# Two small layer-norm operations made on GpSimd instead of VectorE, with a new backlog guard and new order rules in the kernel's own scheduler

## The chip, the cores and the metric

The kernel runs on one core of one Trainium2 chip. The metric is the device time of one launch in microseconds (us), as the median of repeated runs.

The engines are TensorE (PE, with weight loads as PEld), ScalarE (ACT), VectorE (DVE), GpSimd (POOL) and SyncE (SP, which issues transfers).

## The reference, cut to what matters

```python
x = A_x                                          # 1 x 2048 x 640, bf16
xn = _layernorm(x, axis=-1)                      # (x - mean) / sqrt(var + eps)
q = (xn @ wq).reshape(1, 2048, 32, 20)           # 32 heads of 20
k = xn @ wk                                      # one K and one V for all heads
v = xn @ wv
scores = einsum("bhqd,bkd->bhqk", q, k) * 20 ** -0.5
o = einsum("bhqk,bkd->bhqd", softmax(scores), v)
h = relu(xn @ w1 + b1) ** 2
out = x + o_heads_joined @ wo + h @ w2 + b2
```

Nearly all the work is the softmax: 32 heads x 2048 x 2048 scores, which are 2048 tiles of 128 x 512, each of which needs an exponential.

## The kernel before: the parts that the change and the argument touch

The kernel file holds a list scheduler. Every piece of work is an `op` with an engine, an assumed duration, its dependencies and a priority. While the program is built, the scheduler decides in which order each engine gets its operations. The engines then work through fixed queues in that order (a wait of 0.98 us at the head of one is followed up below).

The layer norm of one row tile `st` (128 of the 2048 sequence rows; there are 16 of them, called rows below):

```python
def rows(st):
    p = ROWP[st // 4]
    if st in ACTST:
        ...                                # both statistics passes on ScalarE, small operation on VectorE
    else:
        s1 = op(f"S{st}a", "DVE", 0.40, lambda e: e.bn_stats(...), [x_op[st]], prio=p)
        s2 = op(f"S{st}b", "DVE", 0.40, lambda e: e.bn_stats(...), [x_op[st]], prio=p)
        ag = op(f"AG{st}", "DVE", 0.19, lambda e: e.bn_aggr(...), [s1, s2], prio=p - 0.1)
        ve = op(f"VE{st}", "DVE", 0.08, lambda e: e.tensor_scalar(... scalar1=EPS ... op0=ALU.add), [ag], prio=p - 0.1)
        if st in POOLXN:
            s1 = op(f"NM{st}", "DVE", 0.08, lambda e: e.tensor_scalar(... scalar1=-1.0 ... op0=ALU.mult), [ag], prio=p - 0.1)
    pw = op(f"PW{st}", "POOL", 0.52, lambda e: e.tensor_tensor(... op=ALU.pow), [ve, c_half], lock=True, prio=st // 4)
    eng, dur = ("POOL", 0.87) if st in POOLXN else ("DVE", 0.36)
    xn_op[st] = op(f"XN{st}", eng, dur, lambda e: e.tensor_scalar(...), [pw, s1, x_op[st]], lock=True, prio=p - 0.2)
```

So `VE` adds the epsilon, `NM` negates the mean, `PW` takes the power -1/2 and `XN` normalises. Each normalised row is transposed on TensorE (`T`), copied to SBUF (`TE`), and feeds the products for K, Q and V. Score products (`QK`) need K and Q.

The scores go to one of two consumers. ScalarE takes two or three tiles at a time:

```python
return Op(f"ACT{st_['j']}", "ACT", 0.05 + 0.4267 * n, [lambda e: e.activation(out=PT[...], in_=ps[...], func=AF.Exp, ...)], deps)
```

VectorE and GpSimd take sets of four tiles: one VectorE operation `D1` a tile evicts the score from PSUM as an integer approximation of the exponential, and three more passes a set run on either engine. How many sets there are is not fixed; the scheduler opens a new one (`make_dqk`, `new_set`) when it finds room for it:

```python
def make_dqk(heads):
    opn = [s for s in sets[-NL:] if s["left"]]
    fb = pool_banks()
    if not fb or (len(fb) == 1 and behind()):
        return None
    s = next((s for s in opn if [h for h in s["left"] if h not in heads]), None)
    if s is None:
        if len(opn) >= par("NOPEN"):
            return None
        s = new_set()
```

`par(...)` looks a value up in `RULES`, a table with an entry for stages of 10 us of the schedule. Where TensorE would be idle, the scheduler puts in filler products that compute nothing that is used.

The softmax here doesn't subtract the row's maximum and nothing guards it: scores larger than these inputs give would overflow.

## Time and profile before

| | before |
|---|---|
| time, median of 3 | 705.39 us (705.05 to 706.08) |
| span of the profile | 703.6 us |
| score tiles on ScalarE, on VectorE and GpSimd | 1480, 568 (142 sets) |
| exponentials of 1024, of 1536 columns | 665, 50 |
| first exponential starts | 15.30 us |
| last exponential ends | 695.14 us |
| from there to the end (the tail) | 8.5 us |

The rows of the table come from the timeline and the groups of the trace; the prediction shows the lines. The way to read it: ScalarE's queue of exponentials is one long row without holes. The time is the start of that row, plus its length, plus the tail. A row has a length by count (0.904 us for each 1024-wide exponential, 1.330 us for each 1536-wide one, from start to start) and an excess over it, which I sum from the starts of all exponentials: 3.20 us before 40 us, 8.64 us after it.

### The profile page before, as it was taken

The page shows a single profiled execution, that of the slowest core. Times are in us where ns is not written, and L with a number is a line of the kernel's source. Part 1 is how long each engine was busy: PE and PEld are TensorE (multiplying, and loading weights), DVE is VectorE, ACT ScalarE, POOL GpSimd, SP SyncE. Part 2 cuts the span into 40 slices and gives each one's busy share as a digit, 9 for nine tenths or more (in the row PEclk, how much of TensorE's full clock was granted, in tenths as well). Part 3 has the DMA queues.
Part 4 walks back from the last instruction along what each step waited for, and adds up shares of the span by engine and source line. Part 5 has one row for each costly group of instructions (what it writes and reads, how often), then busy time and mean ns, then how long its engine had stood idle before and what let it go on. Part 6 is the DMA issues. An engine that isn't in the chain of part 4 may idle for free.

```text
span 703.6 us, 22608 instructions
## 1 busy us (share of the span) xinstructions
PE 695.0 (99%) x9780; PEld 216.0 (31%) x9781; DVE 645.9 (92%) x1125; ACT 687.5 (98%) x739; POOL 427.3 (61%) x268
## 2 busy tenths in 40 slices
PE   8999999999999999999999999999999999999997
PEld 4422223233322223332322222323333222233333
DVE  7789999999999998989998998899899999999894
ACT  6899999999999999999999999999999999999995
POOL 4767556567566764666568765766665675644253
PEclk9999999999999999999999999999999999999999
DMA  6325422233337701211101001111112100031201
GB/s 201 98 70 153 115 78 58 81 97 80 84 85 160 162 20 25 55 40 37 52 18 40 23 22 28 29 47 26 46 42 51 36 22 23 20 106 51 55 26 39
DMA packets 42016, 44.00 MB, mean 63 GB/s; under 512 B 15540, under 2 KB 32772, under 8 KB 41788
## 3 DMA queue, kind: packets, MB, share of 16 engines
q1 hardware_dynamic: 39132, 36.93, 19.2%
q0 software_dynamic: 2208, 5.25, 3.9%
q8 instruction: 76, 1.25, 0.7%
q10 hardware_dynamic: 576, 0.38, 0.2%
q14 instruction: 24, 0.20, 0.1%
HBM read 28.03 MB, written 14.91 MB: 61 GB/s over the span
## 4 chain that ended last, share of the span: by engine, by line
ACT 95%; PE 4%; DMA 1%; DVE 0%; SPq 0%; issue 0%; DVEq 0%
ACT PT L910 94%; PE ps L367 3%; DMA x_sb<-in_A_x_dram 1%; PE ps L540 1%; ACT xnT L477 0%; ACT OC L421 0%; DVE out_sb L1164 0%; PE ps L568 0%; SPq L384 0%; ACT OC L422 0%; SPq L391 0%; PE ps L510 0%; PE ps L496 0%; DVEq L227 0%; DVE PT L1164 0%
## 5 line engine op out<-in xcount | busy, mean ns | idle before, releaser
L910 ACT ACTIVATE PT<-ps 128x1024 bf16<-128x1024 f32 (+1 forms) x715 | 677.1, 1219 | 3.8 <-PE ps L367 3.8
L1083 DVE TENSOR_SCALAR tmore<-ps 128x512 uint16<-128x512 f32 x568 | 367.4, 683 | 31.7 <-PE ps L367 28.2
L1101 POOL TENSOR_SCALAR tmore<-tmore 128x2048 uint16<-128x2048 uint16 x109 | 206.4, 1900 | 171.1 <-PE ps L367 62.3
L367 PE MATMUL ps<-qT,kT 20*128 20x512 bf16 x2048 | 281.7, 384 | 1.9 <-ACT PT L910 0.8
L1101 POOL TENSOR_SCALAR x_sb<-tmore 128x2048 uint16<-128x2048 uint16 x100 | 189.3, 1902 | 79.4 <-DVE x_sb L1101 24.2
L367 PEld LDWEIGHTS ps<-qT,kT 20*128 20x128 bf16 x2048 | 71.6, 91 | 280.4 <-ACT PT L910 233.1
L367 PE MATMUL ps<-PT,vx 128*32 128x512 bf16 x1480 | 136.9, 386 | 0.2 <-ACT PT L910 0.2
L1101 DVE TENSOR_SCALAR x_sb<-tmore 128x2048 uint16<-128x2048 uint16 x135 | 96.1, 745 | 0.1
L367 PE MATMUL ps<-x_sb,vxs 128*32 128x512 bf16 x940 | 83.2, 382 | 0.0
L367 PE MATMUL ps<-xnT,w_sb 128*32 128x512 bf16 x960 | 77.2, 384 | 0.1
L367 PE MATMUL ps<-w_sb,big 128*32 128x320 bf16 x1536 | 74.5, 302 | 0.0
L367 PE MATMUL ps<-tmore,vxs 128*32 128x512 bf16 x764 | 69.6, 382 | 0.0
L1101 DVE TENSOR_SCALAR tmore<-tmore 128x2048 uint16<-128x2048 uint16 x82 | 61.5, 770 | 0.1
L367 PE MATMUL ps<-tmore,vx 128*32 128x512 bf16 x568 | 55.7, 382 | 0.0
L367 PEld LDWEIGHTS ps<-PT,vx 128*32 128x32 bf16 x1480 | 34.9, 94 | 62.1 <-issue 53.6
L367 PEld LDWEIGHTS ps<-w_sb,big 128*32 128x32 bf16 x1536 | 32.1, 95 | 29.3 <-issue 22.2
L648 DVE TENSOR_SCALAR hT_tmp<-ps,b1col 128x512 bf16<-128x512 f32 x48 | 35.8, 746 | 3.4 <-PE ps L367 2.7
L367 PE MATMUL ps<-xnT,wq_sb 128*32 128x512 bf16 (+1 forms) x480 | 33.7, 356 | 0.2 <-DVE tmore L1083 0.2
L367 PE MATMUL ps<-wo_c,OC 128*32 128x320 bf16 x608 | 30.9, 301 | 0.0
L367 PEld LDWEIGHTS ps<-x_sb,vxs 128*32 128x32 bf16 x940 | 21.3, 95 | 19.9 <-issue 13.4
L367 PEld LDWEIGHTS ps<-xnT,w_sb 128*32 128x32 bf16 x960 | 17.6, 94 | 26.7 <-issue 22.4
L367 PEld LDWEIGHTS ps<-tmore,vxs 128*32 128x32 bf16 x764 | 18.1, 95 | 16.4 <-issue 11.5
(81 smaller groups left out, 259.4 us busy)
## 6 DMA issues: line engine op xcount, KB each, us to landing
xbd<-b2d SPq DMA_DIRECT2D x16, 320.0 KB, 4.4
xbd<-in_A_x_dram POOLq DMA_DIRECT2D x8, 640.0 KB, 5.8
xr<-xbd SPq DMA_DIRECT2D x32, 160.0 KB, 2.4
w_sb<-in_B_w_dram SPq DMA_DIRECT2D x8, 480.0 KB, 4.4
big<-OR SPq DMA_DIRECT2D x71, 40.0 KB
big<-drs SPq DMA_DIRECT2D x71, 40.0 KB
out_dram<-out_sb SPq DMA_DIRECT2D x15, 160.0 KB, 1.8
qT<-QCr SPq DMA_DIRECT2D x108, 20.0 KB
```

What stands on the lines that cost most here:

```text
L367: return lambda e: e.matmul(out_, l, r, start=start, stop=stop, tile_position=tp)
L540: return [(lambda e, dt=dt: e.transpose(out=psbf(bk)[:, dt * 128:(dt + 1) * 128], in_=xn_sb[:, st, dt:D:DT], identity=ident[:])) for dt in ...
L648: o = Op(f"RL{qc}_{f}", "DVE", 0.66, [lambda e: e.tensor_scalar(out=hT_tmp[:, k % 2, :], in0=ps[:, bk, :], scalar1=b1col[:, f:f + 1], scal ...
L910: return Op(f"ACT{st_['j']}", "ACT", 0.05 + 0.4267 * n, [lambda e: e.activation(out=PT[:, s0:s0 + n, :], in_=ps[:, b0:b0 + (n - 1) * db + ...
L1083: d1 = op(f"D1_{n}_{i}", "DVE", 0.60, lambda e: e.tensor_scalar(out=L[:, cs].bitcast(U16), in0=ps[:, bank, :], scalar1=XA, scalar2=XB, op0 ...
L1101: p = op(f"P{j}_{n}", eng, 0.60 if eng == "DVE" else 1.86, lambda e, T=T, j=j, two=two: e.tensor_scalar(out=T.bitcast(U16), in0=L.bitcast( ...
```

## The change

The intent: VectorE, over 90% busy, is relieved of 18 small operations, GpSimd gets them, the scheduler sees VectorE's backlog before it hands out more tiles (the guard), and the table of order rules is chosen anew for that.

```diff
+DJIT = 9.0
-RULES = {3: {'PVA': 2.1, ...                      # 51 stages, cut
+RULES = {1: {'PVA': 0.95, ...                     # 60 stages, other values, cut
-PRIO = {'NM15': 2.12, 'NM10': 2.88, 'PW2': 0.96}
-NBEF = {'AG4': 10.21, 'NM7': 11.5, 'Qe0_1': 10.11, 'PW12': 25.33}
+PRIO = {'XN1': 0.13}
+NBEF = {'S4a': 6.0, 'AG5': 10.23, 'PW1': 4.94}
-QEACT = (0, 1, 2, 3)
+QEACT = (0, 1)
-FFN0 = 0.3
+FFN0 = 0.6
-ACTST = (2, 5, 6)
-POOLXN = (2, 7, 9, 10, 11, 13, 14, 15)
+ACTST = (0, 2, 4)
+POOLXN = (7, 9, 10, 11, 13, 14, 15)
@@ rows
+            small, pp = (("DVE", 0.08), p - 0.1) if st < 4 else (("POOL", 0.13), st // 4 - 0.5)
-                ve = op(f"VE{st}", "DVE", 0.08, ... prio=p - 0.1)
+                ve = op(f"VE{st}", *small, ... prio=pp)
-                    s1 = op(f"NM{st}", "DVE", 0.08, ... prio=p - 0.1)
+                    s1 = op(f"NM{st}", *small, ... prio=pp)
@@ make_dqk
             if not fb or (len(fb) == 1 and behind()):
                 return None
+            if max(free["DVE"], free["PE"]) + sum(o.dur for o in dve_q if o.frees is not None) > free["PE"] + 0.43 + par("DJIT"):
+                return None
```

The line of `DEFAULTS` that makes `DJIT` known to `par` is left out. `DJIT` is the backlog that the guard allows, `PRIO` and `NBEF` set the priority and the earliest time of single operations, `FFN0` the earliest place of the feed-forward part. `ACTST` are the rows whose statistics ScalarE takes, `POOLXN` those that GpSimd normalises, `QEACT` those whose first Q copy ScalarE makes.

More of the change, by code (lines that the diff above doesn't have):

```diff
@@ L80 @@
 KEEP = 1
-RULES = {3: {'PVA': 2.1, 'PVD': 2.1, 'R3': 1, 'PP': 0.9},
-         4: {'PVA': 2.1, 'PVD': 2.1, 'R3': 1, 'PP': 0.9, 'WARM': 0.78},
-         5: {'D1P': 1, 'MPRIO': 0.5, 'PBIAS': 2.5},
-         6: {'D1P': 1, 'MPRIO': 0.5, 'PBIAS': 2.5, 'ND': 1, 'QKP': 0},
-         7: {'DQP': 2.05, 'URG': 2, 'PVD': 2.1, 'BEHIND': -0.3},
-         8: {'WARM': 0.85, 'DQP': 0.95},
-         10: {'ND': 1, 'NOPEN': 3},
-         11: {'ND': 1, 'NOPEN': 3},
-         12: {'EPS': 0.12},
-         13: {'EPS': 0.06, 'EVP': 0.3},
-         15: {'PBIAS': 0},
-         17: {'EPS': 0.06},
-         18: {'EPS': 0.12},
-         19: {'WARM': 0.78, 'PBIAS': 2.5, 'IDLE': 0.3},
-         21: {'PBIAS': 0, 'KEEP': 0},
-         23: {'EPS': 0.12},
-         25: {'R3': 1, 'EVP': 0.3},
-         26: {'R3': 1, 'EVP': 0.3, 'IDLE': 0.3, 'PVD': 2.1},
-         28: {'EPS': 0.12, 'URG': 3},
-         29: {'EPS': 0.12, 'URG': 3, 'KEEP': 3, 'EVP': 1.1, 'ND': 3},
-         31: {'PBIAS': 1, 'D1P': 1, 'PVD': 1.05},
-         32: {'PBIAS': 1, 'D1P': 1, 'PVD': 1.05, 'DGAP': 0.8, 'DQP': 0.95, 'SQP': 2, 'R3': 1},
-         36: {'PP': 0.9, 'BEHIND': -0.1, 'EVP': 0.3, 'PBIAS': 1.5},
-         37: {'URG': 3, 'JIT': 1.0, 'PVD': 1},
-         38: {'SQP': 0.7, 'URG': 3},
-         39: {'PP': 2.5},
-         40: {'PBIAS': 1},
-         41: {'PBIAS': 1, 'DGAP': 1.5, 'SQP': 0.7},
-         42: {'PBIAS': 1, 'DGAP': 1.5, 'SQP': 2, 'NOPEN': 3, 'ND': 2, 'PVD': 1},
-         43: {'PBIAS': 1, 'DGAP': 1.5, 'SQP': 2, 'NOPEN': 3, 'ND': 2, 'PVD': 1, 'R3': 9},
-         44: {'WARM': 0.78, 'KEEP': 3, 'DLAST': 7.5},
-         45: {'DGAP': 0.8, 'KEEP': 1, 'D1P': 3},
-         48: {'PBIAS': 1},
-         49: {'PBIAS': 1, 'R3': 1},
-         50: {'PBIAS': 1, 'R3': 1},
-         53: {'DLAST': 3.5},
-         54: {'DLAST': 3.5, 'EPS': 0, 'EVP': 0.3},
-         55: {'DLAST': 3.5, 'EPS': 0, 'EVP': 0.3, 'ND': 1},
-         56: {'EVP': 2, 'MPRIO': 1.0},
-         57: {'R3': 1, 'ND': 1},
-         58: {'BEHIND': -0.1, 'EPS': 0, 'PP': 4, 'R3': 1},
-         59: {'BEHIND': -0.1, 'EPS': 0, 'PP': 4, 'R3': 1, 'DRATE': 0.95, 'DLAST': 10, 'PVA': 2.1},
-         60: {'EVP': 1.1},
-         61: {'EVP': 1.1, 'SQP': 0.7},
-         62: {'EVP': 1.1, 'SQP': 0.7, 'KEEP': 3, 'R3': 1, 'NOPEN': 2, 'D1P': 3},
-         64: {'PP': 0.9, 'DRATE': 0.8},
-         65: {'R3': 1},
-         66: {'R3': 1},
-         67: {'EPS': 0.12, 'PVA': 1.05},
-         68: {'R3': 0},
-         69: {'R3': 0, 'JIT': 1.1}}
@@ new lines @@
+DJIT = 9.0
+RULES = {1: {'PVA': 0.95, 'EPS': 0.2, 'DGAP': 0.8},
+         2: {'JIT': 0.9},
+         3: {'JIT': 0.9, 'R3': 0},
+         5: {'EPS': 0.2, 'DJIT': 0.6},
+         6: {'SQP': 2, 'EPS': 0.06},
+         7: {'SQP': 2, 'EPS': 0.06},
+         8: {'DQP': 0.95, 'D1P': 1},
+         9: {'MPRIO': 1.0},
+         10: {'DRATE': 1.1, 'D1P': 1},
+         12: {'R3': 2, 'ND': 1, 'JIT': 1.0, 'MPRIO': 1.1},
+         13: {'NOPEN': 1, 'DRATE': 1.1},
+         14: {'NOPEN': 1, 'DRATE': 1.1, 'KEEP': 2, 'DLAST': 3.5},
+         15: {'R3': 1},
+         16: {'R3': 1, 'DJIT': 1.0, 'ND': 3, 'DRATE': 0.8, 'DGAP': 0.25},
+         17: {'R3': 1, 'DJIT': 1.0, 'ND': 3, 'DRATE': 0.8, 'DGAP': 0.25},
+         18: {'PP': 0.9, 'NOPEN': 1},
+         19: {'PP': 0.9, 'NOPEN': 1, 'EVP': 2, 'SQP': 1.5, 'DJIT': 9},
+         20: {'PP': 4, 'NOPEN': 1, 'EVP': 2, 'SQP': 1.5, 'DJIT': 9},
+         21: {'EVP': 2, 'URG': 2},
+         22: {'JIT': 0.82},
+         23: {'IDLE': 0.2, 'D1P': 3},
+         24: {'IDLE': 0.2, 'D1P': 3, 'PBIAS': 1.5, 'DRATE': 0.95},
+         25: {'DJIT': 0.6, 'DRATE': 0.95, 'URG': 4},
+         26: {'D1P': 1, 'PVA': 2.1, 'DGAP': 0, 'DRATE': 0.95},
+         27: {'JIT': 1.0, 'SQP': 0.7},
+         28: {'EPS': 0.06, 'IDLE': 0.5},
+         29: {'PP': 0.9, 'DRATE': 0.95, 'DLAST': 4.5},
+         30: {'NOPEN': 3, 'DQP': 2.05, 'EPS': 0.12},
+         38: {'DQP': 2.05, 'PBIAS': 2.5},
+         39: {'DQP': 2.05, 'PBIAS': 2.5, 'PP': 2.5, 'IDLE': 0.1, 'ND': 1, 'DRATE': 1.1},
+         40: {'DLAST': 2.5, 'R3': 1, 'EPS': 0.06, 'EVP': 0.3},
+         41: {'DLAST': 2.5, 'R3': 1, 'EPS': 0.03, 'EVP': 0.3, 'DJIT': 0.3},
+         42: {'DLAST': 2.5, 'R3': 1, 'EPS': 0.03, 'EVP': 0.3, 'DJIT': 0.3, 'PBIAS': 0.3},
+         43: {'IDLE': 2, 'DJIT': 9, 'DLAST': 2.5, 'DRATE': 0.95},
+         44: {'IDLE': 2, 'DJIT': 9, 'DLAST': 2.5, 'DRATE': 0.95, 'EPS': 0.12},
+         45: {'IDLE': 2, 'DJIT': 9, 'DLAST': 2.5, 'DRATE': 0.95, 'EPS': 0.12, 'SQP': 0.7, 'BEHIND': -0.3, 'KEEP': 1},
+         46: {'DGAP': 1.5, 'MPRIO': 1.1, 'BEHIND': 0.5},
+         47: {'DGAP': 1.5, 'MPRIO': 0.5, 'BEHIND': 0.5, 'PBIAS': 0.3, 'R3': 1, 'NOPEN': 2},
+         48: {'DGAP': 1.5, 'MPRIO': 0.5, 'BEHIND': 0.5, 'PBIAS': 0.3, 'R3': 1, 'NOPEN': 2, 'D1P': 0.5, 'DRATE': 1.1},
+         49: {'DGAP': 1.5, 'MPRIO': 0.9, 'BEHIND': 0.5, 'PBIAS': 0.3, 'R3': 1, 'NOPEN': 2, 'D1P': 3, 'DRATE': 1.1, 'DLAST': 3.5, 'EVP': 2},
+         50: {'DGAP': 1.5, 'MPRIO': 0.9, 'BEHIND': 0.5, 'PBIAS': 0.3, 'R3': 1, 'NOPEN': 2, 'D1P': 3, 'DRATE': 1.1, 'DLAST': 3.5, 'EVP': 2},
+         51: {'DGAP': 1.5, 'MPRIO': 0.9, 'BEHIND': 0.5, 'PBIAS': 0.3, 'R3': 1, 'NOPEN': 2, 'D1P': 3, 'DRATE': 1.1, 'DLAST': 3.5, 'EVP': 2, 'EPS': 0.06, 'PP': 4},
+         52: {'DGAP': 1.5, 'MPRIO': 0.9, 'BEHIND': 0.5, 'PBIAS': 2.5, 'R3': 1, 'NOPEN': 2, 'D1P': 1, 'DRATE': 1.1, 'DLAST': 3.5, 'EVP': 2, 'EPS': 0.06, 'PP': 4, 'SQP': 0.7, 'URG': 4},
+         53: {'DGAP': 1.5, 'MPRIO': 0.9, 'BEHIND': 0.5, 'PBIAS': 2.5, 'R3': 1, 'NOPEN': 2, 'D1P': 1, 'DRATE': 1.1, 'DLAST': 3.5, 'EVP': 1.1, 'EPS': 0.06, 'PP': 2.5, 'SQP': 0.7, 'URG': 4},
+         54: {'DGAP': 1.5, 'MPRIO': 0.9, 'BEHIND': 0.5, 'PBIAS': 2.5, 'R3': 1, 'NOPEN': 2, 'D1P': 1, 'DRATE': 1.1, 'DLAST': 3.5, 'EVP': 1.1, 'EPS': 0.06, 'PP': 2.5, 'SQP': 0.7, 'URG': 6, 'KEEP': 3},
+         55: {'DGAP': 1.5, 'MPRIO': 0.9, 'BEHIND': 0.5, 'PBIAS': 2.5, 'R3': 1, 'NOPEN': 2, 'D1P': 1, 'DRATE': 1.1, 'DLAST': 3.5, 'EVP': 1.1, 'EPS': 0.06, 'PP': 2.5, 'SQP': 0.7, 'URG': 6, 'KEEP': 3},
+         56: {'JIT': 0.82, 'MPRIO': 0.9, 'PP': 2.5},
+         57: {'JIT': 0.82, 'MPRIO': 0.9, 'PP': 2.5, 'WARM': 0.85, 'R3': 1, 'SQP': 0.7},
+         58: {'JIT': 0.82, 'MPRIO': 0.9, 'PP': 2.5, 'WARM': 0.85, 'R3': 1, 'SQP': 0.7},
+         59: {'DLAST': 4.5},
+         60: {'DLAST': 4.5, 'NOPEN': 2, 'MPRIO': 1.0},
+         61: {'DLAST': 4.5, 'NOPEN': 2, 'MPRIO': 1.0},
+         62: {'R3': 0, 'WARM': 0.78},
+         63: {'R3': 0, 'WARM': 0.78, 'NOPEN': 1, 'URG': 2},
+         64: {'R3': 0, 'WARM': 0.78, 'NOPEN': 1, 'URG': 2},
+         65: {'R3': 0, 'WARM': 0.78, 'NOPEN': 1, 'URG': 2},
+         66: {'R3': 0, 'WARM': 0.78, 'NOPEN': 1, 'URG': 2, 'D1P': 1, 'ND': 2, 'MPRIO': 0.9, 'DQP': 0.95},
+         67: {'R3': 9, 'WARM': 0.78, 'NOPEN': 1, 'URG': 2, 'D1P': 1, 'ND': 2, 'MPRIO': 0.9, 'DQP': 0.95},
+         68: {'R3': 9, 'WARM': 0.78, 'NOPEN': 1, 'URG': 2, 'D1P': 0.5, 'ND': 2, 'MPRIO': 0.9, 'DQP': 0.95, 'PBIAS': 1},
+         69: {'R3': 0, 'WARM': 0.78, 'NOPEN': 1, 'URG': 2, 'D1P': 0.5, 'ND': 2, 'MPRIO': 0.9, 'DQP': 0.95, 'PBIAS': 1}}
@@ L159 @@
 DEFAULTS = dict(EVP=EVP, PBIAS=PBIAS, MPRIO=MPRIO, DGAP=DGAP, DLAST=DLAST, DRATE=DRATE, BEHIND=BEHIND, IDLE=IDLE, URG=URG, NOPEN=NOPEN,
-                EPS=0.03, JIT=JIT, R3=R3, STATIC=STATIC, PVA=1, PVD=1, D1P=1, PP=4, SQP=2, DQP=3, QKP=0, ND=2, WARM=WARM, KEEP=KEEP)
+                EPS=0.03, JIT=JIT, R3=R3, STATIC=STATIC, PVA=1, PVD=1, D1P=1, PP=4, SQP=2, DQP=3, QKP=0, ND=2, WARM=WARM, KEEP=KEEP, DJIT=DJIT)
 class Ctr:
@@ L428, in rows @@
                 ag = op(f"AG{st}", "DVE", 0.19, lambda e: e.bn_aggr(out=mv[:, st, :], in_=stats6[:, st, :, :].rearrange("p a b -> p (a b)")), [s1, s2], prio=p - 0.1)
-                ve = op(f"VE{st}", "DVE", 0.08, lambda e: e.tensor_scalar(out=mv[:, st, 1:2], in0=mv[:, st, 1:2], scalar1=EPS, scalar2=None, op0=ALU.add), [ag], prio=p - 0.1)
+                ve = op(f"VE{st}", *small, lambda e: e.tensor_scalar(out=mv[:, st, 1:2], in0=mv[:, st, 1:2], scalar1=EPS, scalar2=None, op0=ALU.add), [ag], prio=pp)
                 opm = ALU.subtract
                 if st in POOLXN:
-                    s1 = op(f"NM{st}", "DVE", 0.08, lambda e: e.tensor_scalar(out=mv[:, st, 0:1], in0=mv[:, st, 0:1], scalar1=-1.0, scalar2=None, op0=ALU.mult), [ag], prio=p - 0.1)
+                    s1 = op(f"NM{st}", *small, lambda e: e.tensor_scalar(out=mv[:, st, 0:1], in0=mv[:, st, 0:1], scalar1=-1.0, scalar2=None, op0=ALU.mult), [ag], prio=pp)
                     opm = ALU.add
```

## The prediction

> **What bounds the kernel now.** I read four views in this order: the page's busy table, its chain of waits, the groups by shape, and the timeline of ScalarE over the first 40 us.
>
> ```profile
> span 703.6 us, 22608 instructions
> PE 695.0 (99%) x9780; PEld 216.0 (31%) x9781; DVE 645.9 (92%) x1125; ACT 687.5 (98%) x739; POOL 427.3 (61%) x268
> ...
> ACT 95%; PE 4%; DMA 1%; DVE 0%; SPq 0%; issue 0%; DVEq 0%
> ```
>
> Three engines are over 90% busy, so the busy table doesn't decide. The chain does: 95% of the span is ScalarE, nearly all of it on one line, the softmax exponential from PSUM to SBUF. So, up to a start and a tail, the time is the length of ScalarE's queue of exponentials.
>
> ```profile
> L910 ACT ACTIVATE PT<-ps 128x1024 bf16<-128x1024 f32 x665 | 621.9, 1190 | 1.4 <-PE ps L367 1.4
> L1083 DVE TENSOR_SCALAR tmore<-ps 128x512 uint16<-128x512 f32 x568 | 367.4, 683 | 31.7 <-PE ps L367 28.2
> ...
> L910 ACT ACTIVATE PT<-ps 128x1536 bf16<-128x1536 f32 x50 | 79.0, 1609 | 2.3 <-PE ps L367 2.3
> ...
> L429 DVE TENSOR_SCALAR mv<-mv 128x1 f32<-128x1 f32 x13 | 1.9, 146 | 0.1
> ...
> L432 DVE TENSOR_SCALAR mv<-mv 128x1 f32<-128x1 f32 x7 | 1.0, 145 | 0.0
> ```
>
> The groups by shape show how the 2048 score tiles of 128x512 are shared: ScalarE takes 665x2 + 50x3 = 1480, and VectorE with GpSimd takes 568 by an integer approximation (142 sets of 4). The idle column shows that ScalarE waits 3.7 us in total. The timeline shows where:
>
> ```profile
> 9.78 0.83 ACT L422 ACTIVATE OC<-x_sb,mv 128x640 bf16<-128x640 bf16 x1
> ...
> 10.75 0.74 ACT L421 ACTIVATE OC<-x_sb 128x640 bf16<-128x640 bf16 x1
> ...
> 11.54 1.30 ACT L477 ACTIVATE xnT<-ps 128x640 bf16<-128x640 bf16 x2
> ...
> 15.30 12.46 ACT L910 ACTIVATE PT<-ps 128x1024 bf16<-128x1024 f32 x13 [1.05 <-PE ps L367]
> 28.15 1.94 ACT L910 ACTIVATE PT<-ps 128x1024 bf16<-128x1024 f32 x2 [0.39 <-PE ps L367]
> 32.44 8.29 ACT L910 ACTIVATE PT<-ps 128x1536 bf16<-128x1536 f32 x8 [2.35 <-PE ps L367]
> ```
>
> All of it lies before 32.44 us. Until then the layer norm, the transposes and the K projections have to supply scores, and ScalarE outruns them. The first two rows are layer-norm statistics that stand in ScalarE's queue ahead of the copies of rows 2 and 3 (a row here is one of the 16 tiles of 128 sequence rows). From 32.44 us to the last exponential at 693.9 us there is no gap.
>
> The starts of the 715 exponentials give the cadence. The median spacing is 0.904 us after a 1024-wide one and 1.331 us after a 1536-wide one. 665 x 0.904 + 50 x 1.33 = 667.7 us. All spacing over those figures adds to 11.8 us: about 3.0 us are the two stalls above (the start column shows more than the idle column because recorded spans overlap), and 8.8 us are spread evenly, some 0.5 us in each 40 us. The last exponential's record ends at 695.1 us, and 8.5 us of tail follow: the last P x V product, its normalisation, output projection and store.
>
> [...] (1331 - 904) ns over 512 elements is 0.834 ns. [...] here PE shows 99% and is on the chain for only 4%. [...]
>
> **The change part by part.** The instruction order of both programs, without times, gives the counts.
>
> *Small layer-norm operations.* 11 epsilon adds and 7 negations leave VectorE for GpSimd: 18 x 0.146 = 2.6 us of recorded VectorE time, but in the timeline such an operation displaces the next by only 0.06 to 0.12 us, so some 1.6 us. They all lie before 29 us. On GpSimd they cost about 18 x 0.13 = 2.3 us (an estimate, between its 0.09 to 0.12 us memsets and the 0.15 us on VectorE), where the engine is often idle. Each row also saves a hop: epsilon and power are now on one engine, and the hop from epsilon to power measures 0.23 us from start to start. In steady state this part is worth nothing.
>
> *Start order.* The layer norms of rows 0 to 3 are now done ahead of most other statistics, and ScalarE copies all four transposed rows back to back. Before, row 3 was normalised at 9.96 us behind the statistics of rows 4 and 7, and its copy ended at 12.84 us. Walking the new order with the old durations, by hand: x of rows 1 and 3 can be used by VectorE from about 3.8 and 4.6 us; the four normalisations fall at about 7.05, 7.6, 8.0 and 9.2 us (rows 3, 0, 1, 2); ScalarE's fifth statistics pass starts at 7.88 us, when its rows land, and the four copies then run from 8.7 to about 11.2 us. The K, Q and V products of four rows are PE work of 0.88 us each, most of it after row 2's transpose; they end near 13.4 us. First scores at 13.4 us instead of 14.87, first exponential near 13.85 us instead of 15.30: **1.4 us earlier**.
>
> *Stalls of the start.* The new order has K for rows 4 to 7 as one piece after 16 score tiles, followed by V and two transposes (1.2 + 0.6 + 0.8 us); before, it was broken up by score tiles. By the same walk ScalarE now waits some 1.7 us there, and about 1.0 us more after 30 tiles for the next K piece. That is 2.7 us in place of 3.0 us. So the earlier start is kept, hardly more.
>
> *Share of tiles.* The new program has 669 exponentials of 1024 and 50 of 1536: 1488 tiles on ScalarE, 560 on VectorE. Four more exponentials: 4 x (0.904 + 0.012 usual spread) = **+3.7 us** on the path. VectorE loses 8 evictions at 0.68 us and 12 passes at about 0.75 us, GpSimd gains 6 passes at 1.90 us (two sets fewer are 6 passes fewer in all): VectorE is eased by 14 us, off the path. PE does 6 products of 0.22 us fewer and 10 fillers more, off the path too.
>
> *Guard and rules.* A new guard holds back VectorE's score tiles when its backlog of evictions is long. It and the stage rules only reorder the steady part, where ScalarE already never waits; they can win at most the 8.8 us of spread, and I expect less than 1.5 us either way. The tail has the same order of work, 8.5 us.
>
> Sum: 705.4 - 1.4 - 0.3 + 3.7 = 707.4. The rules were chosen for this order, so I grant 0.6 us more of start-up stall or spread, a choice and not a reading: **706.8 us**.
>
> **Rivals.** First: the start wins more. If both K stalls vanish too, 2.7 us more come off: about 704. For it: 18 small operations leave a VectorE that has almost no idle time from 10 to 28 us. Against it: [...] its K, V and transpose pieces stand in one run there. Second: VectorE's relief takes jitter out of the steady part; half of 8.8 us would give about 702.5. For it: VectorE is at 92% and the guard aims at it. Against it: the spread is even over 660 us, which looks like a fixed hand-over cost, not like queues. Third: the new order opens a new wait, on GpSimd in the start (its powers, negations and normalisations now queue behind each other) or in a stage where K or P x V comes late; one such hole costs 1 to 4 us: 708 to 711. For it: rows 7, 9, 10 and 11 now each have four GpSimd steps in series, and the first K pieces need them.
>
> **Range and chances.** None of these reaches the 14.1 us that 2% means: winning it would need every stall, the whole spread and the earlier start at once, with the extra tiles free. Range 703.2 to 710.2 us. Faster by over 2%: 0.01; within 2%: 0.98; slower: 0.01.
>
> **What would show each step.** Right: the first exponential near 13.9 us; 719 exponentials at the same 0.904 and 1.331 us; ScalarE still over 94% of the chain; a stall near 21 to 23 us and one near 30 us; no gap over 0.3 us later; a tail of 8.5 us; epsilon rows on GpSimd near 0.13 us. Wrong: a first exponential later than 15 us, stalls over 4 us or under 1 us, a spread that differs from 8.8 us by more than 2 us, or idle time of ScalarE after 40 us.

The sum: 705.4 - 1.4 - 0.3 + 3.7 = 707.4 us, less the 0.6 us granted to chosen rules, is 706.8 us. Nothing was charged for moving work between VectorE and GpSimd; that zero was not shown.

## The result, and the profile after

| | before | after |
|---|---|---|
| time, median of 3 | 705.39 us (705.05 to 706.08) | 709.93 us (709.76 to 710.06) |
| span of the profile | 703.6 us | 708.0 us |
| tiles on ScalarE | 1480 | 1488 |
| first exponential starts | 15.30 us | 13.72 us |
| excess before 40 us | 3.20 us | 4.86 us |
| excess after 40 us | 8.64 us | 8.77 us |
| last exponential ends | 695.14 us | 699.01 us |
| tail | 8.5 us | 9.0 us |

The changed kernel takes 1.0062 times the time of before, 95% interval 1.0040 to 1.0085: by the 2% limit the same, though slower beyond doubt.

The span grew by 4.4 us, and the rows of the table give where it went: the first exponential 1.58 us earlier, the excess of the start 1.66 us longer, that of the rest 0.13 us longer, the count of exponentials 3.66 us more (by the cadence and the longer record of the last one), and the tail 0.53 us longer. -1.58 + 1.66 + 0.13 + 3.66 + 0.53 = 4.40.

The page of the changed kernel, the busy table and the chain of waits:

```profile
span 708.0 us, 22589 instructions
PE 697.3 (98%) x9787; PEld 218.5 (31%) x9788; DVE 634.3 (90%) x1090; ACT 691.3 (98%) x741; POOL 442.0 (62%) x291
...
ACT 89%; PE 7%; DVE 1%; POOL 1%; DMA 0%; issue 0%; DVEq 0%
```

VectorE became 12 us less busy (the prediction had 14 us from the tiles and 1.6 to 2.6 us from the small operations), and it bought nothing. ScalarE's share of the chain fell to 89%, but that is no new bound: the listing of the chain's pieces has one stretch from 262.9 to 287.7 us that runs over TensorE, because there ScalarE came to wait for a moment (the only gap after 40 us over 0.3 us is one of 0.42 us), and here the chain, once it had stepped over to busy TensorE, stayed on it for 24.7 us. Where two engines are both almost full, the share of the chain says little; the holes in the row of exponentials say more.

The groups by shape of the changed kernel (columns: count, busy us and mean ns of one, idle time of the engine before them):

```profile
L921 ACT ACTIVATE PT<-ps 128x1024 bf16<-128x1024 f32 x669 | 625.9, 1184 | 3.4 <-PE ps L377 3.2
...
L921 ACT ACTIVATE PT<-ps 128x1536 bf16<-128x1536 f32 x50 | 79.4, 1622 | 2.1 <-PE ps L377 2.1
...
L440 POOL TENSOR_SCALAR mv<-mv 128x1 f32<-128x1 f32 x11 | 2.5, 226 | 4.6 <-DVE nk L501 2.3 <-DVE mv L439 1.8
...
L443 POOL TENSOR_SCALAR mv<-mv 128x1 f32<-128x1 f32 x7 | 1.6, 229 | 0.6
```

The 719 exponentials are those that the instruction order had shown. The 18 small operations took 226 and 229 ns on GpSimd, where VectorE took 146 and 145 ns and where the scheduler (and my estimate) had 130 ns. On GpSimd the next operation starts 0.17 to 0.35 us after such a one (timeline of the changed kernel); on VectorE, where nothing is waited for, it starts 0.02 to 0.12 us after (timeline of the kernel before). ScalarE's idle time before exponentials went from 3.7 to 5.5 us. The timeline of ScalarE shows where (columns: start us, length us, what, idle time before it and what ended it):

```profile
8.24 1.87 ACT L488 ACTIVATE xnT<-ps 128x640 bf16<-128x640 bf16 x3
...
13.72 7.44 ACT L921 ACTIVATE PT<-ps 128x1024 bf16<-128x1024 f32 x8 [1.43 <-PE ps L377]
22.90 1.94 ACT L921 ACTIVATE PT<-ps 128x1024 bf16<-128x1024 f32 x2 [1.74 <-PE ps L377]
25.19 4.67 ACT L921 ACTIVATE PT<-ps 128x1536 bf16<-128x1536 f32 x4 [0.35 <-PE ps L377]
31.58 9.17 ACT L921 ACTIVATE PT<-ps 128x1536 bf16<-128x1536 f32 x9 [1.72 <-PE ps L377]
```

The stalls, counted from start to start against the cadence, are 1.86 us before 22.90 us, 0.47 us before 25.19 us and 1.83 us before 31.58 us. Before the change they were 0.54 and 2.46 us.

For the last of them I followed the wait backwards. ScalarE waits for scores; those wait for the K product of rows 8 to 11 on TensorE, which needs the copies of rows 10 and 11 from VectorE. TensorE's, VectorE's and GpSimd's timelines there:

```profile
28.81 1.26 PE L377 MATMUL ps<-xnT,wk_c 128*20 128x512 bf16 x20 [0.48 <-DVE xnT L554]
```

```profile
27.12 0.45 DVE L447 TENSOR_SCALAR big<-x_sb,mv,rstd 128x640 bf16<-128x640 bf16 x1 [0.98 <-POOL rstd L445]
...
27.88 0.87 DVE L554 COPY xnT<-ps 128x640 bf16<-128x640 bf16 x2
```

```profile
25.25 0.87 POOL L447 TENSOR_SCALAR big<-x_sb,mv,rstd 128x640 bf16<-128x640 bf16 x1
26.21 0.23 POOL L440 TENSOR_SCALAR mv<-mv 128x1 f32<-128x1 f32 x1
26.52 0.57 POOL L445 TENSOR_TENSOR rstd<-mv,nhalf 128x1 f32<-128x1 f32 x1
```

The transposes that the copies read run on TensorE from 26.37 to 27.12 us. In VectorE's queue row 12's normalisation stands ahead of the copies; it waits 0.98 us for row 12's power, until 27.12 us, and the first copy follows only at 27.88 us. GpSimd comes to that power late because its epsilon addition (0.23 us, and 0.31 us from its start to the power's) lies ahead of it in a queue that is full from 21.1 to 29.3 us. Row 12 isn't needed for these K products at all. This is the head-of-line wait of a fixed queue: an operation that nobody needs yet holds up two that are needed.

### The profile page after: what moved, and what is told of

It reads as the page before. It is cut to its first block, busy times and chain, and to the rows that moved or that the text cites. A ratio compares the mean times of both kernels' runs of the same rounds, so it can differ in the third digit from the quotient of the medians.

```text
span 708.0 us, 22589 instructions
## 1 busy us (share of the span) xinstructions
PE 697.3 (98%) x9787; PEld 218.5 (31%) x9788; DVE 634.3 (90%) x1090; ACT 691.3 (98%) x741; POOL 442.0 (62%) x291
## 4 chain that ended last, share of the span: by engine, by line
ACT 89%; PE 7%; DVE 1%; POOL 1%; DMA 0%; issue 0%; DVEq 0%
ACT PT L921 89%; PE ps L377 6%; DMA x_sb<-in_A_x_dram 0%; PE ps L551 0%; POOL rstd L445 0%; DVE big L447 0%; PE ps L579 0%; DVE OR L438 0%; DVE xnT L554 0%; DVE out_sb L1177 0%; DVE OR L437 0%; PE ps L521 0%; PE ps L486 0%; POOL big L447 0%; PE ps L507 0%
## 5 line engine op out<-in xcount | busy, mean ns | idle before, releaser
L1096 DVE TENSOR_SCALAR tmore<-ps 128x512 uint16<-128x512 f32 x560 | 362.6, 683 | 37.7 <-PE ps L377 33.0
L1114 POOL TENSOR_SCALAR tmore<-tmore 128x2048 uint16<-128x2048 uint16 x107 | 202.3, 1898 | 151.8 <-DVE tmore L1114 40.9
L1114 POOL TENSOR_SCALAR x_sb<-tmore 128x2048 uint16<-128x2048 uint16 x108 | 203.8, 1897 | 89.0 <-DVE x_sb L1114 41.5
L377 PE MATMUL ps<-PT,vx 128*32 128x512 bf16 x1488 | 139.3, 386 | 0.9 <-ACT PT L921 0.6
L1114 DVE TENSOR_SCALAR x_sb<-tmore 128x2048 uint16<-128x2048 uint16 x124 | 87.3, 732 | 0.0
```

Of the source, the lines that this page charges most:

```text
L377: return lambda e: e.matmul(out_, l, r, start=start, stop=stop, tile_position=tp)
L1096: d1 = op(f"D1_{n}_{i}", "DVE", 0.60, lambda e: e.tensor_scalar(out=L[:, cs].bitcast(U16), in0=ps[:, bank, :], scalar1=XA, scalar2=XB, op0 ...
L1114: p = op(f"P{j}_{n}", eng, 0.60 if eng == "DVE" else 1.86, lambda e, T=T, j=j, two=two: e.tensor_scalar(out=T.bitcast(U16), in0=L.bitcast( ...
```

## The experiments

Twelve kernels ran, all with correct results. In their rounds the kernel before took 705.21 to 705.63 us.

### e1: the small operations back on VectorE, all else as in the changed kernel

The order of the changed kernel is kept (`order_all` is the finished list of the scheduler); only the engine of these operations is put back after the scheduler has run.

```diff
+        for o in order_all:
+            if o.name[:2] in ("VE", "NM"):
+                o.eng = "DVE"
```

> The changed kernel, its order kept, with only the 18 small operations (11 epsilon adds, 7 negations) put back on VectorE at the same places. Theory (they cost 0.23 us each on GpSimd instead of the 0.13 the order was made with, so GpSimd falls behind, row 12's normalisation on VectorE waits for it 0.98 us at 26.1 us and holds up the copies of rows 10 and 11 behind it): that wait goes, the 15th exponential starts near 30.6 us instead of 31.58, the time falls by 0.7 to 1.2 us to about 709.0. Rival (VectorE is the limit of the start, the move relieves it): the 18 operations cost VectorE 1 to 1.5 us before 30 us, the 15th exponential starts at 31.6 to 33 us, the time is 709.9 to 711.5.

Measured: 710.07 us (709.55 to 711.17), ratio 1.0065 to before, interval 1.0052 to 1.0078. The time is that of the changed kernel; the gain that I expected isn't seen in it. The 15th exponential starts at 32.38 us instead of the expected 30.6. By these numbers it is the rival's forecast, but not for the rival's reason: row 12's normalisation no longer waits, and the excess before 40 us is 4.05 us instead of 4.86. Of these 0.8 us, 0.55 are in the last stall (1.28 us instead of 1.83) and 0.17 in the first. So the operations cost at most 0.8 us of stall where they were put: ScalarE started 1.58 us later in this profile, for another reason, and a later start may by itself give the rows more time to arrive (e9 and e11 below, whose orders differ by six fillers alone, start 2.12 us apart and differ by 0.40 us in the excess). The 0.55 us are firmer, because e2 below, with its small operations on GpSimd, has the same stall of 1.28 us once row 12 is out of the way. The late start of the profiled run, the slowest of the five, has this cause:

```profile
7.62 1.25 PE L486 MATMUL ps<-ident,big 128*128 128x128 bf16 x10 [1.79 <-DVE big L447]
```

```profile
8.00:12.00 4.00, 3.96 (x57) 2.46 (x59) 2.66 (x9) 2.38 (x6) 0.55 (x1) 0.57 0.75 272
```

The second line is the table by stretches, from 8 to 12 us: busy time of PE, PEld, DVE, ACT and POOL, then the granted clock of TensorE as a share of full speed, which is 0.57 here (it is 1.00 in the changed kernel's profile). TensorE had stood idle for 1.79 us before the first transposes, then ran at half its clock for 3.4 us (a mean of 0.57 over four us is 3.4 us at 0.5 and 0.6 at full clock), and the first exponential came at 15.30 us instead of 13.72. The idle gap is itself in part chance. The same eight filler products ahead of it, in the changed kernel and in e1:

```profile
3.20 3.48 PE L521 MATMUL ps<-hT_tmp,OR 128*128 128x512 bf16 x8
```

```profile
3.20 2.64 PE L521 MATMUL ps<-hT_tmp,OR 128*128 128x512 bf16 x8
```

In e1's profile the eight took 2.64 us instead of 3.48, so the fillers ran out sooner. But this tells of one run only: the four others, with a mean clock of 1.000, took 709.55 to 710.22 us, and the three of the changed kernel 709.76 to 710.06. So the half clock explains the slowest run and not why the median shows no gain; by time e1 doesn't confirm the 0.8 us, and why stays open.

### e2: row 12's normalisation behind the two copies

```diff
+        x12 = next(o for o in order_all if o.name == "XN12")
+        order_all.remove(x12)
+        k12 = 1 + next(k for k, o in enumerate(order_all) if o.name == "TE11")
+        for o in order_all[:k12]:
+            o.deps = [d for d in o.deps if d is not x12]
+        order_all.insert(k12, x12)
```

> The changed kernel with one instruction moved: row 12's normalisation on VectorE stands behind the copy of row 11 instead of in front of the copy of row 10. Small operations stay on GpSimd. Theory (an in-order queue with a waiting instruction ahead of a needed one): VectorE has no 0.98 us wait, the K product of rows 8 to 11 starts about 0.9 us earlier (near 27.9 us), the 15th exponential near 30.7 us, time about 709.0. Rival (GpSimd's own normalisations of rows 10 and 11 come late and set the K product): K product still near 28.8 us, time 709.9 within 0.3.

Measured: 709.85 us (709.40 to 710.70), ratio 1.0062, interval 1.0049 to 1.0074. VectorE's and TensorE's timelines of this run:

```profile
27.25 0.89 DVE L554 COPY xnT<-ps 128x640 bf16<-128x640 bf16 x2 [0.35 <-PE ps L551]
28.06 0.44 DVE L447 TENSOR_SCALAR big<-x_sb,mv,rstd 128x640 bf16<-128x640 bf16 x1
```

```profile
28.63 1.26 PE L377 MATMUL ps<-xnT,wk_c 128*20 128x512 bf16 x20
```

The copies no longer wait for GpSimd, so the hold-up was read rightly, but they now wait for TensorE's transposes, and the K product comes right behind other TensorE work, at 28.63 us and not at 27.9 as expected. By its numbers this is the rival's forecast too, though what sets the product is TensorE's queue and not GpSimd's normalisations. From first exponential to the one behind the last stall it is 17.32 us instead of 17.86: 0.54 us gained, where the removed wait was 0.98 us. This run's first exponential was 0.36 us later than that of the changed kernel, because a row of x landed later (a ScalarE pass at 8.22 instead of 7.50 us), and the time is the same within the noise. When one wait is removed, the next one behind it, here TensorE's own queue, is what is left.

### e3: the move alone, in the kernel before

```diff
+        for o in order_all:
+            if o.name[:2] == "NM" or o.name[:2] == "VE" and int(o.name[2:]) >= 4 and int(o.name[2:]) not in ACTST:
+                o.eng = "POOL"
```

> The kernel before, its order kept, with only the same kind of operations (epsilon of the ten rows from 4 on that VectorE has statistics of, and all negations) moved to GpSimd: the move alone, without the new start, shares and rules. First exponential unchanged at 15.30 us. Theory (the move lengthens the chain of each row on GpSimd by about 0.3 us an operation and relieves a VectorE that is not what the stall waits for): stall before 32.44 us equal or longer by 0 to 1.5 us, time 705.4 to 706.9. Rival (VectorE's relief is worth its 1.5 us): time near 704.

Measured: 705.99 us (705.62 to 706.70), ratio 1.0007, interval 0.9993 to 1.0021. The stall in the start, before the exponential at 32.62 us of this run, grew by 0.27 us, and nothing shrank: the excess before 40 us is 3.53 us instead of 3.20, after it 8.61. The move by itself is worth nothing, and perhaps costs 0.3 us. The relief of VectorE isn't on the path.

### e4 and e5: the kernel before with 140 and with 138 sets

```diff
@@ new_set, the kernel before
+            if len(sets) >= 140:                  # 138 in e5
+                return None
```

> The kernel before with one condition more: no set of approximate tiles after the 140th, so ScalarE has 1488 tiles as in the changed kernel (660 exponentials of 1024, 56 of 1536). Start, small operations, guard and rules are those of before; only the last two blocks differ. Theory (the share is the largest term): 660 x 0.904 + 56 x 1.330 = 671.1 us of exponentials in place of 667.7, first exponential still near 15.3 us, time 705.5 + 3.5 = 709.0 us, within 0.6. Rival (share is hidden, the whole loss is made in the start): time within 0.7 of 705.5.

> As the last, with 138 sets: 1496 tiles, 725 exponentials (679 of 1024, 46 of 1536). 679 x 0.904 + 46 x 1.330 = 675.0 us. Theory: 705.5 + 7.3 = 712.8 us within 0.8. Rival (share hidden): 705.5 within 1.

The exponentials of e4:

```profile
L910 ACT ACTIVATE PT<-ps 128x1024 bf16<-128x1024 f32 x660 | 616.3, 1191 | 1.4 <-PE ps L367 1.4
...
L910 ACT ACTIVATE PT<-ps 128x1536 bf16<-128x1536 f32 x56 | 86.4, 1644 | 2.4 <-PE ps L367 2.4
```

Measured: 709.05 us with 140 sets (708.66 to 709.32, ratio 1.0046, interval 1.0033 to 1.0058) and 713.17 us with 138 (713.15 to 713.34, ratio 1.0106, interval 1.0090 to 1.0121). Nothing else of the change is in these kernels. With the changed kernel's share of 140 sets the kernel before loses 3.4 of the 4.5 us. The cadence gives the same: e4 has 660 x 0.904 + 56 x 1.330 = 671.1 us of exponentials, before has 667.7. And e5, with 679 x 0.904 + 46 x 1.330 = 675.0 us, should lose 7.3 us and lost 7.5. Each set that ScalarE has to take over costs 1.7 to 1.9 us; none of it is hidden.

### e6 and e7: the changed kernel without its guard, and with the old rules

```diff
@@ e6
-            if max(...) + sum(...) > free["PE"] + 0.43 + par("DJIT"):
+            if max(...) + sum(...) > free["PE"] + 0.43 + 99.0:
@@ e7
-RULES = {1: {'PVA': 0.95, ...
+RULES = {3: {'PVA': 2.1, ...                      # the whole table of the kernel before
```

> The changed kernel with its new guard (no score tile for VectorE while its evictions are in arrears) never biting; rules, start and small operations stay. The scheduler then makes 134 sets: 1512 tiles, 723 exponentials. Theory (rules and guard were chosen together; the guard by itself takes nothing from the time, but rules made for another order leave fewer sets and holes): first exponential near 13.7 to 14.1 us, time 719 to 726 us, ScalarE's idle time after 40 us some microseconds. Rival (the guard costs tiles, without it VectorE takes more): time under 709 us.

> The changed kernel with the table of order rules of the kernel before in place of its own. The scheduler makes 136 sets, 735 exponentials. Theory (a rule table fits one order only): time 719 to 727 us, holes in ScalarE's queue after 40 us of more than 4 us in sum. Rival (the new rules are what costs the 4.5 us): time near 705 us.

One look at each: 721.75 us and 727.00 us. Their shares are 134 and 136 sets, which follows from their exponentials in the trace: 657 x 2 + 66 x 3 = 1512 tiles, and 699 x 2 + 35 x 3 + 1 = 1504. In e7 there are holes in the steady part too (excess after 40 us 15.7 us instead of 8.8). The counts and the holes add up: by the cadence e6 has 14.0 us more of exponentials than before, 3.9 us more excess, and a first exponential 1.6 us earlier, together 16.3 us, which is what its span has over that of before (719.9 and 703.6 us). For e7 it is 11.2 us of exponentials, 9.7 us of excess and a first exponential 0.6 us later, and its span is 21.6 us longer. (TensorE's mean clock from 20 to 40 us was 0.83 in e7's profile, so part of its excess may be the clock's.) The two runs say that guard, rules and order can't be judged by being taken out one at a time; that the rules were chosen with the rest in place is the likely reason, not a tested one. Why the whole change comes to 140 sets, where the old order with its own rules has 142, no run shows.

### e8 and e9: the kernel before with a searched start

To see whether a better start is to be had, I let an annealing search reorder the first 45 us of the kernel before, with the scheduler's own durations, and put the two best orders on the chip. No operation is added or removed.

```diff
+        START = {
+            "PE": (9, [12, 9, 10, 11, 14, 13, 15, ...]),      # new order of the first operations, cut
+            "ACT": (9, [10, 9, 13, ...]),
+            "DVE": (10, [11, 10, 12, ...]),
+            "POOL": (11, [12, 11, 13, ...]),
+        }
+        for g, (lo, p) in START.items():
+            s = sq[g]                              # the queue of one engine
+            s[lo:lo + len(p)] = [s[i] for i in p]
+        ...                                        # the queues are merged into one list again, cut
```

> The kernel before, with the operations of its first 45 us only put in another order on TensorE, ScalarE, VectorE and GpSimd (found by an annealing search over the scheduler's own durations and latencies, which has the last exponential 1.4 us earlier; the 142 sets and all operations are unchanged). If the end is set by ScalarE's queue from the first exponential on, and nothing else, a gain in the start goes through to the end one to one: 715 exponentials as before, first near 15.2 us, the excess before 40 us down from 3.2 to about 1.8 us, the steady excess 8.6 us, and 704.2 us. The rival: the assumed durations of the small operations and the hand-overs are too short (as on GpSimd in the changed kernel), the tightly packed start slips on the chip, the excess stays at 3.0 us or more, and the time is 705.4 to 706.5 us.

> As the run before, a second result of the same search, with 1.15 us less by the scheduler's own durations. Gain goes through: 704.5 us, excess before 40 us 2.0 us. Slips on the chip: 705.4 to 706.5 us.

Measured: 707.17 us (705.63 to 709.31, ratio 1.0028, interval 1.0014 to 1.0042) and 707.46 us (705.27 to 709.15, ratio 1.0030, interval 1.0014 to 1.0045). Slower, and over three times as scattered as the kernel before (704.97 to 706.00 in the same rounds). The excess before 40 us is 3.18 us in e8 and 2.90 in e9, so the searched gain isn't there, as the rival had it for e8, but the times lie above the rival's as well. TensorE's timeline and the stretches of e8's profile show one cause:

```profile
7.08 0.47 PE L475 MATMUL ps<-ident,big 128*128 128x128 bf16 x5 [2.16 <-DVE big L436]
```

```profile
8.00:12.00 4.00, 4.00 (x56) 2.14 (x55) 3.07 (x15) 3.15 (x7) 1.83 (x4) 0.63 0.67 246
```

In e8 the search had moved fillers, which for a model without a clock are good for nothing, out of the first microseconds. TensorE stood idle for 2.16 us, and the clock was at half for 3.4 us (0.79 from 7 to 8 us, then 0.50, 0.50 and 0.51 up to 11 us), while the first transposes and the first K product ran. First exponential: 16.15 us, in e9 (also with a stretch at half clock, 0.50 from 10 to 13 us) 16.50, instead of 15.30. The gap alone doesn't tell: one of 1.79 us (e1) and this one were followed by half clock, while after one of 1.80 us in e5 the clock is 1.00 up to 40 us. Why, no run here shows.

The other runs show that this isn't all. In e9 the three runs with a mean clock of 0.997 took 707.80 to 709.15 us and the other three 705.27 to 707.12, which fits. In e8 only the profiled run shows a lowered clock (0.998, 707.15 us); the other five, at 0.999 and 1.000, took 705.63 to 709.31. So the half clock is not what makes e8 slow in its median, and that cause stays open.

### e10 and e11: the same two starts with fillers put back

```diff
+        for name, n in [("T0", 5)]:               # e11: [("T0", 2), ("K0", 4)]
+            t0 = named[name]
+            k = next(i for i, o in enumerate(sq["PE"]) if o is t0)
+            more = [Op("fill", "PE", 0.215, warm_parts(), [c_ones, c_zero]) for _ in range(n)]
+            ...
+            sq["PE"][k:k] = more
```

> The kernel of e8 with five more filler products on TensorE ahead of the first transpose, where e8 left TensorE idle for 2.16 us and its clock then stood at half for 3.4 us. If the half clock is what spoilt e8, this run has full clock from 5 to 20 us, a first exponential between 14.5 and 15.5 us, an excess before 40 us below 3.2 us and a time of 703.8 to 704.8 us. The rival, that the searched order slips on the chip by itself because its durations are too short: first exponential or stalls as late as in e8, 705.5 to 707.5 us even at full clock.

> The kernel of e9 with two fillers more ahead of the first transpose and four behind the second, where TensorE stood idle for 0.56 and 1.12 us and its clock then fell to half. Clock theory: full clock, first exponential between 14.8 and 15.5 us instead of 16.5, 704.0 to 705.0 us. Rival (the order itself slips): 705.5 to 707.5 us. If the last output issue again lies beside an instruction packet, the tail is 10.5 instead of 8.5 us and 2 us are to be added in either case.

Measured: 705.86 us (705.35 to 707.07, ratio 1.0002, interval 0.9988 to 1.0015) and 705.48 us (704.98 to 706.65, ratio 1.0002, interval 0.9989 to 1.0014). In both profiles the clock is full from 7 to 40 us. (The table of stretches shows 1.00 before that too, but the fillers don't run as at full clock there: up to 5.3 us in e10 and to 5.8 us in e11 they start 0.43 us apart, and by 6.2 us 0.22 us apart. In every profile of this case the first fillers have that doubled spacing; that it is the half clock is my reading.) The median of e10 is 1.3 us lower than that of e8, and that of e11 2.0 us lower than that of e9, with more work that computes nothing. How much of it the clock is, the medians don't say, for e8 least of all, and in the second figure tails play a part: the profile of e9 has a tail of 10.5 us, that of e11 one of 8.9 (more on tails below). In e11 the first exponential starts at 14.38 us. In e10 it starts at 15.77 us, later than I had expected: its profiled run was the slowest of the five, with a row of x that came late. So I count from the ScalarE pass that waits for that row to the first exponential: e10 takes 7.22 us (from 8.55) where e8 takes 8.31 (from 7.84), and e11 7.19 us (from 7.19) where e9 takes 8.76 (from 7.74). So the half clock cost some 1.1 to 1.6 us in these profiles, an estimate from these differences.

But neither beats the kernel before: e10's time lies in the rival's range, e11's between the two, and the excess before 40 us is 3.17 and 3.30 us. At full clock, too, the searched orders don't bring the gain that the scheduler's durations promised. e11's last exponential ends 0.36 us earlier than before (694.78 us; first exponential -0.92, excess of the start +0.10, excess of the rest +0.46), and its tail is 8.9 us instead of 8.5. That took me to the tail.

### e12: the changed kernel with twelve filler products fewer

The tail of the changed kernel is 0.53 us longer than before, although from the end of the last exponential to the end of VectorE's last eviction both traces have 6.03 us. What differs is SyncE's issue of the output stores. Before:

```profile
699.98 1.30 SPq L708 DMA_DIRECT2D out_dram<-out_sb  x3
701.33 0.45 SPq L708 DMA_DIRECT2D out_dram<-PT  x1
```

After, three issues take 1.81 us instead of 1.30:

```profile
703.84 1.81 SPq L719 DMA_DIRECT2D out_dram<-out_sb  x3
705.70 0.46 SPq L719 DMA_DIRECT2D out_dram<-PT  x1
```

The queues of the transfers name a suspect. Before and after, in the page's list of queues:

```profile
q8 instruction: 76, 1.25, 0.7%
```

```profile
q8 instruction: 77, 1.26, 0.7%
```

Queue 8 moves instructions by the page's own label, 16 KB a packet (1.25 MB in 76). The changed kernel has one packet more, and by its record it starts at 703.80 us and takes 1.0 us, beside the three issues; before, the last packet starts at 695.89 us. By number the packets go with TensorE's instructions: 76 for the 9780 + 9781 = 19,561 recorded before, 77 for the 9787 + 9788 = 19,575 after, some 255 to a packet, while no other engine has more than 1125 recorded. Two of the 76 come in the first 20 us and the last at 695.89 us. So I took them for TensorE's program, fetched while it runs: an inference from counts and times, which e12 puts to the test.

Over the profiles of both kernels and of the first eleven experiments a packet beside the issues and long issues went together each time. In seven a packet overlaps the issues, and they are long: 1.63 to 2.24 us for the group of three, or, in e9, 2.22 us for the fourth alone. In the other six the three take 1.30 to 1.34 us; three of these six also have 77 packets, but the last is over before the stores begin, so it is the place that counts. The tails go with it: 8.50 to 8.54 us in these six profiles, 8.85 to 10.51 us in the seven. To test it I took three filler operations near 600 and 614 us out of the changed kernel, 24 TensorE instructions, so that the 77th packet wouldn't be needed.

```diff
+        gone = [o for o in order_all if o.name == "fill" and 600 < o.start < 650]
+        for o in gone:
+            order_all.remove(o)
```

> The changed kernel without three of its filler operations (twelve products of zeros on TensorE near 600 and 614 us, where ScalarE never waits), so that TensorE has some 24 instructions fewer than the changed kernel and 10 fewer than the kernel before. If the longer tail comes from a 16 KB instruction packet of TensorE's stream that lands beside the output stores, queue 8 shows 76 packets instead of 77, none after 697 us, the three output issues take 1.3 us instead of 1.8, the tail after the last exponential is 8.5 instead of 9.0 us, and the time 709.4 us instead of 709.9. If the longer tail has another cause, the issues stay at 1.8 us and the time at 709.9 us.

The issues of e12, and its queue:

```profile
703.95 1.30 SPq L719 DMA_DIRECT2D out_dram<-out_sb  x3
705.30 0.45 SPq L719 DMA_DIRECT2D out_dram<-PT  x1
```

```profile
q8 instruction: 76, 1.25, 0.7%
```

Measured: 709.37 us (709.27 to 710.89), ratio 1.0060, interval 1.0047 to 1.0074. 76 packets, issues of 1.30 us, a tail of 8.51 us, all else of the start and the steady part as in the changed kernel (excess 4.84 and 8.77 us). One detail was off: the last packet came at 700.19 us, not before 697, but with no store beside it. The median is 0.56 us lower than that of the changed kernel, from other rounds. The intervals of the ratios overlap, but the four runs of e12 with a mean clock of 1.000 took 709.27 to 709.74 us (the fifth, at 0.998, 710.89) and the three of the changed kernel, all at 1.000, 709.76 to 710.06. So the trace shows the 0.5 us of the tail, and the time agrees with it.

## Why the prediction was right, and where it was off

The class was right (the same, by the limit of 2%), and 709.9 us lies in the range, by 0.3 us. The sum was 3.1 us short: 2.0 of that are the stalls of the start (0.3 us less forecast, 1.66 us more measured), 0.6 the gain granted to chosen rules, 0.5 the tail. By its own steps:

- **What bounds the kernel: right.** Counts and cadence of ScalarE's queue gave all of the sum's large terms. e4 and e5 show it by the share alone.
- **First exponential: right.** 13.85 us walked by hand, 13.72 measured. How close it came is partly luck: three other profiles with this start (e2, e6, e12) have 13.66 to 14.09 us.
- **Share of tiles: right.** +3.7 us; measured +3.66 in the traces, and +3.4 by e4, which has the same 140 sets.
- **Steady part: right.** The excess stayed (8.64 and 8.77 us), the relief of VectorE by 12 us bought nothing there.
- **Stalls of the start: this step failed.** "That is 2.7 us in place of 3.0 us", a gain of 0.3; the excess of the start rose by 1.66 us. The first stall was as walked (1.7 us and 1.86 measured); the second was 1.83 us, not 1.0, and one of 0.47 us had not been seen. The prediction had named stalls over 4 us as a sign that it is wrong; from start to start they sum to 4.16 us. What the walk had left out is the small operations' time on GpSimd, mis-sized as "about 18 x 0.13" where 226 to 229 ns were measured, in a GpSimd queue that is full just then, and what waits behind it on VectorE. Put back on VectorE (e1) the excess falls by 0.8 us, of which 0.55 in the last stall are backed by e2 and the rest may be the later start of that profile. The other half of the miss, or more, comes with the order itself: with the small operations back, the excess of the start is still 4.05 us. I didn't isolate more of it; e2 shows that behind the first hold-up TensorE's own queue comes next.
- **"Each row also saves a hop": true, and worth nothing.** e3 shows no gain of the move alone; that the longer operations ate what the hop saved is my reading, not a test.
- **The 0.6 us that I granted to chosen rules: not there.** It was a wish in the sum, and it had the wrong sign.
- **The tail of 8.5 us: off by 0.5 us.** "The same order of work" was right, and yet the tail grew, by a cause that lies in the length of TensorE's program (e12).
- **The rivals.** The third, a new wait on GpSimd in the start, 708 to 711 us, is what came, in kind and in size, though at most 0.8 us of it is shown to be GpSimd's doing. The first, that both K stalls vanish, and the second, that the spread shrinks, did not.

What stays open: a version with the changed kernel's early start and the old share of 142 sets, the rest of the stalls in the changed start, and the times of e1 and e8. Neither the scheduler, with some search over the rules, nor the searched starts gave one that beats 705.4 us.

## What to carry to other kernels

When one engine's queue is the time, count its instructions first: here 8 tiles more on ScalarE explain most of the loss, and 12 us less work on a neighbour that was 92% busy explain nothing. Moving small operations to a quieter engine needs their measured duration there (here 226 to 229 ns instead of 145 to 146) and a look at that engine's queue at that moment, because a wait at the head of a fixed queue stops what stands behind it (0.98 us on VectorE here, gone in e2). And a start or a tail of a few microseconds is ruled by things that this scheduler doesn't model, such as a halved TensorE clock (3.4 us at half after idle gaps of 1.79 us in e1 and 2.16 us in e8), a late row (a ScalarE pass at 8.22 instead of 7.50 us in e2), or an instruction packet beside the last stores (1.81 us of issues in the changed kernel instead of 1.30). So look at several profiles before you believe a gain of under one microsecond, and look at the clocks of the runs that were not profiled before you explain their median by the one that was.
